# Float32 attention and gated feed-forward on one core: the even chunks of w_gate, their parts at two offsets in SBUF and their products in another order

## The chip, the cores and the metric

One core of a Trainium2 chip runs the whole program. The metric is the device time of one execution in microseconds; the median of three runs stands for the kernel. The profile comes from one further execution, whose own time is given beside its span.

## The reference

Attention with a mask by blocks of 64 positions (a query sees its own block and all earlier ones), then a feed-forward layer with a SiLU gate on its output, all compared in float32:

```python
# q, k, v: (8, 8, 576, 64); x: 4608 tokens of 512; w_gate, w_val: (512, 1536); w_out: (1536, 512)
scores = np.where(mask, scale * np.matmul(q, k.transpose(0, 1, 3, 2)), -1000000000.0)
attn = np.exp(scores - np.max(scores, axis=-1, keepdims=True))
attn = attn / (np.sum(attn, axis=-1, keepdims=True) + 1e-09)
x = np.matmul(attn, v)             # heads laid side by side: 4608 x 512
g = x @ w_gate
silu = g * (1.0 / (1.0 + np.exp(-g)))
out = (silu * (x @ w_val)) @ w_out
```

The weights arrive as float64.

## The kernel before

**Numbers in two parts.** TensorE multiplies here in the type fp32r, which keeps fewer bits than float32. So each factor is kept as a high part (the rounded value) and a low part (what rounding took off), and each product of the feed-forward layer is three matmuls into one PSUM sum: high weights by high x, high weights by low x, low weights by high x. In w_gate and w_val the weights are the stationary operand, loaded into the array before each matmul, and x is the moving one, streamed through it.

**Weights in SBUF (L200 to L212).** w_gate and w_val stay in SBUF for the whole run, cut into 12 chunks of 128 columns of d_ff. `g_odd` holds w_gate's odd chunks, `v_all` all of w_val, `g_even` w_gate's even chunks; each is a pair of tiles, number 0 for the high parts and number 1 for the low parts. A tile has 128 partitions, and along a partition 4 pieces d of the 512 input dimensions by its columns. `w_at(which, x, i)` gives part x of chunk i of w_gate (which = 0) or w_val (which = 1). Tiles take their places in the order of their calls. A tile of 64 bytes that nobody uses, `gap`, stands ahead of `g_even`. As it comes out, g_odd and v_all begin 64 bytes past a multiple of 128 (1984, 14272, 26560, 51136), both g_even tiles at a multiple of 128 (75776, 88064), and x's parts `xhl`, w_out's parts `wo` and the hidden layer's parts `hhl` too. Every step between the pieces that a matmul reads is a multiple of 128.

**The feed-forward loop.** Tokens are taken in 18 tiles of 256. For each tile, `feed_forward` walks over d_ff two chunks at a time, an even one and the odd one behind it. `up(i, 0, ...)` makes w_gate's products into one PSUM bank `gv`: 12 matmuls for the even chunk (y = 0; 4 pieces d, 3 matmuls each: L1105 high by high, L1106 high by low, L1107 low by high), then 12 for the odd one (y = 1). `up(i, 1, ...)` makes the same 24 for w_val into the other bank. ACT takes a tanh of the gate's sums (L1139), DVE makes the gated product (L1142 and the next) and ACT and DVE split it into `hhl` (L1152, L1155). The products with w_out (`down`, L1197 to L1199) are 12 matmuls of 512 columns into the sum `po`, with `hhl` stationary and `wo` moving. A turn of this loop is thus even 12, odd 12, value 24, w_out 12 (those of the turn before), with attention's matmuls (L569, L653, L782) between turns.

**The order of the work.** A planner in the kernel (`in_order`) gives every step an estimated cost and a rank and writes one fixed order for each engine. A step of `up` is one chunk's 12 matmuls from tile 4 on (`j >= FINE`); for tiles 0 to 3 it is the 3 matmuls of one d, so that other work can come between them, since weights and x are still being prepared. A step is placed only when its chunk's low part, the last thing made of a weight chunk (DVE, L986), and x's low part are done. Six pieces of w_out live for a time in w_gate's and w_val's tiles (`AWAY`) and are multiplied from there for tiles 0 and 1.

Of the kernel before, what the change touches and what calls it, by code (L numbers as in the profile page):

```python
# [7 lines left out]
F32 = mybir.dt.float32  # L8
F32R = mybir.dt.float32r
# [9 lines left out]
def kernel(  # L19
# [17 lines left out]
    nc = tc.nc  # L37
# [3 lines left out]
    P = 128  # L41
# [5 lines left out]
    NDC = DM // P  # L47
# [47 lines left out]
    const = ctx.enter_context(tc.tile_pool(name="const", bufs=1))  # L95
# [54 lines left out]
    def add(engine, cost, rank, fn, after=(), bufs=(), port=False, mode="", stage=""):  # L150


        t = Task(engine, cost, rank, fn, after, bufs, port, mode)
        for a in after:
            if a is not None:
                a.next.append(t)
                t.waits += 1
        for u in bufs:
            u.left += 1
        t.n, t.stage = len(tasks), stage  # L160
        tasks.append(t)
        return t
# [8 lines left out]
    def up_us(n):  # L171
        return n * 0.1134 + (0.012 if n < 3 * NDC else 0.0)
# [29 lines left out]
    half_w, whole_w = [P, NDC, DFF // 2], [P, NDC, DFF]  # L202
    g_odd = [const.tile(half_w, F32R, name=f"g_odd{x}") for x in range(2)]
    v_all = [const.tile(whole_w, F32R, name=f"v_all{x}") for x in range(2)]
    const.tile([P, 16], F32, name="gap")
    g_even = [const.tile(half_w, F32R, name=f"g_even{x}") for x in range(2)]

    def w_at(which, x, i):

        if which:  # L210
            return v_all[x][:, :, i * P : (i + 1) * P]
        return (g_odd if i % 2 else g_even)[x][:, :, i // 2 * P : (i // 2 + 1) * P]  # L212
# [101 lines left out]
    for i in range(7):  # L314
        n = 2**i
# [755 lines left out]
    def feed_forward(j, t0, w, xs):  # L1071
# [16 lines left out]
        def rank(i):  # L1088
            return (10.0 + (t0 + w * i / NFC) / S) if j > 1 else SIDE[j] + w * i / NFC / S

        def up(i, which, prev):

            ps = Buf("gv")
            ts = up_done[0]
            for y in range(2):

                for ds in [range(NDC)] if j >= FINE else [[d] for d in range(NDC)]:

                    def products(ds=ds, y=y):
                        hi, lo = (w_at(which, k, i + y) for k in range(2))  # L1100
                        o = ps[0][:, y * w : (y + 1) * w]
                        for d in ds:
                            xhi, xlo = (xs[d][1][k] for k in range(2))
                            first, last = d == 0, d == NDC - 1
                            nc.tensor.matmul(o, lhsT=hi[:, d], rhs=xhi[:, 0:w], start=first, stop=False)  # L1105
                            nc.tensor.matmul(o, lhsT=hi[:, d], rhs=xlo[:, 0:w], start=False, stop=False)  # L1106
                            nc.tensor.matmul(o, lhsT=lo[:, d], rhs=xhi[:, 0:w], start=False, stop=last)  # L1107

                    ts = add(
                        "PE",  # L1110
                        up_us(3 * len(ds)),
                        rank(i),
                        products,
                        [ts, *(xs[d][0] for d in ds), w_done[i + y, which]],
                        [ps, *(xs[d][1] for d in ds)],
                        stage="up",
                    )
                    ts.prev = prev
                    prev = ts if j >= FINE else None
            chain["up"] = up_done[0] = ts  # L1120
            return ps, ts

        for i in range(0, NFC, 2):
# [11 lines left out]
            n = 2 * w  # L1135
# [46 lines left out]
            every = [(y, m) for y in range(2) for m in range(nb)]  # L1182
# [273 lines left out]
```

## Time and profile before

| what | value |
|---|---|
| runs | 1172.72, 1174.53, 1175.42 us; median 1174.53 |
| profiled execution | 1178.6 us, span 1176.7 us, mean granted clock 0.991 |
| PE busy | 1149.6 us, 98% of the span, 8578 matmuls |
| weight loads (PEld) | 1029.6 us, 88%, 8578 |
| DVE, ACT, POOL busy | 746.6, 625.0, 322.1 us |
| DMA | 197.41 MB, mean 168 GB/s |

Rows of the profile name a line of the kernel, the engine, the operation and the tiles: `gv<-xhl,g_even` writes PSUM tile gv from x's parts and the weights g_even. Numbers of buffers are left out, so g_even stands for its high and its low tile. PE is the stream of matmuls, PEld the loads of their stationary operand, which run beside earlier matmuls. The length of a matmul's record includes its way through the array and overlaps that of the next, so PE's pace is read from one start to the next, not from lengths.

### The profile page before, as it was taken

Reading aid. Unit: us, or ns where it says so; the run is one execution under the profiler, and the core shown is the slowest. Engines: PE = TensorE matmul, PEld = TensorE weight load, DVE = VectorE, ACT = ScalarE, POOL = GpSimd, SP = SyncE. Lnnn points to the kernel's source line nnn. Section 1 sums busy time; section 2 is a strip of 40 time slices with the busy share of each in tenths; the row PEclk is TensorE's granted clock in tenths of the full one; section 3 lists DMA queues with packets and bytes.
Section 4 is the critical chain, followed back from the end, with each engine's and each line's share of the span. In section 5 each row is a group of like instructions: output and inputs, shape, how many; then the busy total and the mean of one; then the engine's idle time right before and its main releaser. Section 6 shows DMA issues by size and latency. Waiting matters only on the chain.

```text
span 1176.7 us, 21979 instructions
## 1 busy us (share of the span) xinstructions
PE 1149.6 (98%) x8578; PEld 1029.6 (88%) x8578; DVE 746.6 (63%) x1230; ACT 625.0 (53%) x1114; POOL 322.1 (27%) x139
## 2 busy tenths in 40 slices
PE   6889999999999999999999999999999999999998
PEld 5567878888899998989899998989989898999997
DVE  5798889677678574768567674856648565423222
ACT  5788877646383655637374564637355463212111
POOL 3212100144523333422414332342424233000000
PEclk8899999999999999999999999999999999999999
DMA  7666858756574646755376544745556434654442
GB/s 202 168 169 189 208 178 259 190 175 175 162 180 134 172 143 172 210 176 129 132 201 199 146 150 134 216 140 163 157 161 192 166 108 148 199 160 133 146 166 103
DMA packets 266984, 197.41 MB, mean 168 GB/s; under 512 B 195264, under 2 KB 231376, under 8 KB 266880
## 3 DMA queue, kind: packets, MB, share of 16 engines
q1 hardware_dynamic: 264304, 195.29, 56.8%
q8 instruction: 67, 1.10, 0.4%
q10 hardware_dynamic: 2576, 0.72, 0.3%
q14 instruction: 37, 0.30, 0.1%
HBM read 171.57 MB, written 24.38 MB: 167 GB/s over the span
## 4 chain that ended last, share of the span: by engine, by line
PE 90%; DVE 3%; ACT 3%; DMA 2%; issue 1%; SPq 0%; POOL 0%; ACTq 0%; POOLq 0%; DVEq 0%
PE gv L1105 17%; PE gv L1107 16%; PE gv L1106 16%; PE po L1197 8%; PE po L1198 7%; PE po L1199 7%; PE at L782 7%; PE at L569 5%; PE at L653 1%; PE at L1197 1%; PE at L442 1%; PE at L1198 1%; PE at L1199 1%; DVE mx L710 1%; DMA qk<-in_k_dram 1%
## 5 line engine op out<-in xcount | busy, mean ns | idle before, releaser
L714 POOL PARTITION_ALL_REDUCE mx<-mx x80 | 141.0, 1811 | 441.7 <-DVE mx L710 131.6
L833 POOL PARTITION_ALL_REDUCE mx<-mx x48 | 178.5, 3766 | 229.1 <-DVE mx L710 210.0
L1105 PE MATMUL gv<-xhl,v_all 128*128 128x256 f32 x864 | 241.0, 279 | 0.0
L1107 PE MATMUL gv<-xhl,v_all 128*128 128x256 f32 x864 | 239.2, 277 | 0.0
L1106 PE MATMUL gv<-xhl,v_all 128*128 128x256 f32 x864 | 239.0, 277 | 0.0
L1142 DVE SCALAR_TENSOR_TENSOR t<-t,gv 128x512 f32<-128x512 f32 x108 | 73.8, 684 | 146.6 <-ACT t L1139 146.0
L1105 PEld LDWEIGHTS gv<-xhl,v_all 128*128 128x128 f32 x864 | 162.1, 188 | 3.4 <-issue 2.1
L1106 PEld LDWEIGHTS gv<-xhl,v_all 128*128 128x128 f32 x864 | 162.3, 188 | 0.8
L1155 DVE TENSOR_TENSOR hhl<-t,hhl 128x512 fp32r<-128x512 f32 x108 | 91.4, 847 | 112.3 <-ACT hhl L1152 109.0
L1107 PEld LDWEIGHTS gv<-xhl,v_all 128*128 128x128 f32 x864 | 162.2, 188 | 0.1
L1152 ACT CAST hhl<-t 128x512 fp32r<-128x512 f32 x108 | 67.3, 623 | 156.2 <-PE po L1198 114.4
L1197 PE MATMUL po<-wo,hhl 128*128 128x512 f32 x372 | 148.3, 399 | 0.7 <-ACT ob L1224 0.7
L1198 PE MATMUL po<-wo,hhl 128*128 128x512 f32 x372 | 145.6, 391 | 0.0
L1199 PE MATMUL po<-wo,hhl 128*128 128x512 f32 x372 | 145.3, 390 | 0.0
L738 DVE TENSOR_TENSOR sc<-sc,mx 128x640 f32<-128x640 f32 (+6 forms) x168 | 123.4, 774 | 20.4 <-POOL mx L714 20.4
L1139 ACT ACTIVATE t<-gv 128x512 f32<-128x512 f32 x108 | 64.6, 598 | 119.6 <-PE gv L1107 116.9
L1105 PE MATMUL gv<-xhl,g_even 128*128 128x256 f32 x432 | 124.2, 288 | 0.2 <-DVE t L1142 0.2
L742 ACT ACTIVATE sc<-sc 128x1024 f32<-128x1024 f32 (+3 forms) x104 | 105.8, 1030 | 32.5 <-DVE sc L738 31.4
L1106 PE MATMUL gv<-xhl,g_even 128*128 128x256 f32 x432 | 122.5, 283 | 0.0
L1107 PE MATMUL gv<-xhl,g_even 128*128 128x256 f32 x432 | 122.3, 283 | 0.0
L1105 PE MATMUL gv<-xhl,g_odd 128*128 128x256 f32 x432 | 120.4, 279 | 0.0
L1107 PE MATMUL gv<-xhl,g_odd 128*128 128x256 f32 x432 | 119.5, 277 | 0.4 <-DVE g_odd L986 0.4
(175 smaller groups left out, 2398.8 us busy)
## 6 DMA issues: line engine op xcount, KB each, us to landing
wo<-wo_d SPq DMA_DIRECT2D x200, 512.0 KB
out_dram<-ob SPq DMA_DIRECT2D x35, 256.0 KB
v<-in_v_dram SPq DMA_DIRECT2D x64, 128.0 KB
xt<-x_d SPq DMA_DIRECT2D x64, 128.0 KB
rt<-r_d SPq DMA_DIRECT2D x128, 64.0 KB
qk<-in_q_dram SPq DMA_DIRECT2D x112, 72.0 KB
qk<-in_k_dram SPq DMA_DIRECT2D x104, 72.0 KB
x_d<-xu SPq DMA_DIRECT2D x24, 288.0 KB
```

Of the source, the lines that this page charges most:

```text
L714: nc.gpsimd.partition_all_reduce(m, m, channels=P, reduce_op=bass_isa.ReduceOp.max)
L738: nc.vector.tensor_tensor(piece(c), scores_of(c), m, ALU.subtract)
L742: nc.scalar.activation(x, x, AF.Exp)
L782: nc.tensor.matmul(ps[0][own(x), 1 - i if sums else i, q0 - s0 : s1 - s0], lhsT=ones if sums else vt[0][:, 2 * lane + c, own(x)], rhs=sc[0 ...
L833: nc.gpsimd.partition_all_reduce(m, m, channels=P, reduce_op=bass_isa.ReduceOp.add)
L1105: nc.tensor.matmul(o, lhsT=hi[:, d], rhs=xhi[:, 0:w], start=first, stop=False)
L1106: nc.tensor.matmul(o, lhsT=hi[:, d], rhs=xlo[:, 0:w], start=False, stop=False)
L1107: nc.tensor.matmul(o, lhsT=lo[:, d], rhs=xhi[:, 0:w], start=False, stop=last)
L1155: nc.vector.tensor_tensor(hh[1][:, 0:n], t[0][:, 0:n], hh[0][:, 0:n].bitcast(F32), ALU.subtract)
L1197: nc.tensor.matmul(po, lhsT=hi, rhs=whi, start=i + y == 0, stop=False)
L1198: nc.tensor.matmul(po, lhsT=hi, rhs=wlo, start=False, stop=False)
L1199: nc.tensor.matmul(po, lhsT=lo, rhs=whi, start=False, stop=i + y == NFC - 1)
```

## The change

The tiles of w_gate's even chunks change places, with two more 64-byte tiles between and behind them, and for the even chunks the third kind of matmul (low weights by high x) of all pieces d of a step goes ahead of the others:

```diff
     const.tile([P, 16], F32, name="gap")
-    g_even = [const.tile(half_w, F32R, name=f"g_even{x}") for x in range(2)]
+    low = const.tile(half_w, F32R, name="g_even1")
+    const.tile([P, 16], F32, name="gap1")
+    g_even = [const.tile(half_w, F32R, name="g_even0"), low]
+    const.tile([P, 16], F32, name="gap2")
...
-                        for d in ds:
-                            xhi, xlo = (xs[d][1][k] for k in range(2))
-                            first, last = d == 0, d == NDC - 1
-                            nc.tensor.matmul(o, lhsT=hi[:, d], rhs=xhi[:, 0:w], start=first, stop=False)
-                            nc.tensor.matmul(o, lhsT=hi[:, d], rhs=xlo[:, 0:w], start=False, stop=False)
-                            nc.tensor.matmul(o, lhsT=lo[:, d], rhs=xhi[:, 0:w], start=False, stop=last)
+                        low_first = which == 0 and y == 0
+                        every = [(d, x) for d in ds for x in range(3)]
+                        if low_first:
+                            every.sort(key=lambda p: p[1] < 2)
+                        for n, (d, x) in enumerate(every):
+                            first, last = ds[0] == 0 and not n, ds[-1] == NDC - 1 and n == len(every) - 1
+                            nc.tensor.matmul(
+                                o,
+                                lhsT=(lo if x == 2 else hi)[:, d],
+                                rhs=xs[d][1][int(x == 1)][:, 0:w],
+                                start=first,
+                                stop=last,
+                            )
```

The low tile now lies at 75776, a multiple of 128, the high tile at 88128, 64 bytes past one. g_odd and v_all stay where they were; everything behind g_even moves up by 128 bytes, so xhl, wo and hhl remain at multiples of 128. The costs and ranks that the planner works with are the same, and so is the order of all steps: on DVE, ACT, POOL and SP every instruction stands where it stood.

On PE the twelve matmuls of an even chunk change their order. This is the last even chunk of the last tile, before. Behind the arrow stand the moving tile (`xhl4_0` is the high part of x's first piece, `xhl4_1` its low part, and so on to xhl7) and the stationary one (g_even0 high, g_even1 low):

```order
L1105 MATMUL gv1_0_179<-xhl4_0_100,g_even0_76 128x256
L1106 MATMUL gv1_0_179<-xhl4_1_101,g_even0_76 128x256
L1107 MATMUL gv1_0_179<-xhl4_0_100,g_even1_77 128x256
L1105 MATMUL gv1_0_179<-xhl5_0_102,g_even0_76 128x256
L1106 MATMUL gv1_0_179<-xhl5_1_103,g_even0_76 128x256
L1107 MATMUL gv1_0_179<-xhl5_0_102,g_even1_77 128x256
L1105 MATMUL gv1_0_179<-xhl6_0_104,g_even0_76 128x256
L1106 MATMUL gv1_0_179<-xhl6_1_105,g_even0_76 128x256
L1107 MATMUL gv1_0_179<-xhl6_0_104,g_even1_77 128x256
L1105 MATMUL gv1_0_179<-xhl7_0_106,g_even0_76 128x256
L1106 MATMUL gv1_0_179<-xhl7_1_107,g_even0_76 128x256
L1107 MATMUL gv1_0_179<-xhl7_0_106,g_even1_77 128x256
```

And the same twelve places of the changed kernel, on PE too (all matmuls of `up` are now on L1111):

```order
L1111 MATMUL gv1_0_181<-xhl4_0_102,g_even1_76 128x256
L1111 MATMUL gv1_0_181<-xhl5_0_104,g_even1_76 128x256
L1111 MATMUL gv1_0_181<-xhl6_0_106,g_even1_76 128x256
L1111 MATMUL gv1_0_181<-xhl7_0_108,g_even1_76 128x256
L1111 MATMUL gv1_0_181<-xhl4_0_102,g_even0_78 128x256
L1111 MATMUL gv1_0_181<-xhl4_1_103,g_even0_78 128x256
L1111 MATMUL gv1_0_181<-xhl5_0_104,g_even0_78 128x256
L1111 MATMUL gv1_0_181<-xhl5_1_105,g_even0_78 128x256
L1111 MATMUL gv1_0_181<-xhl6_0_106,g_even0_78 128x256
L1111 MATMUL gv1_0_181<-xhl6_1_107,g_even0_78 128x256
L1111 MATMUL gv1_0_181<-xhl7_0_108,g_even0_78 128x256
L1111 MATMUL gv1_0_181<-xhl7_1_109,g_even0_78 128x256
```

The four low weights have moved to the front, one after the other; the eight with high weights follow in their old order.

In tiles 0 to 3, where a step has one d, the move stays within three matmuls. Two such steps that follow each other on PE, of tile 0 (pieces d = 1 and 2), before:

```order
L1105 MATMUL gv0_0_157<-xhl1_0_94,g_even0_76 128x256
L1106 MATMUL gv0_0_157<-xhl1_1_95,g_even0_76 128x256
L1107 MATMUL gv0_0_157<-xhl1_0_94,g_even1_77 128x256
L1105 MATMUL gv0_0_157<-xhl2_0_96,g_even0_76 128x256
L1106 MATMUL gv0_0_157<-xhl2_1_97,g_even0_76 128x256
L1107 MATMUL gv0_0_157<-xhl2_0_96,g_even1_77 128x256
```

The same two steps on PE in the changed kernel:

```order
L1111 MATMUL gv0_0_159<-xhl1_0_96,g_even1_76 128x256
L1111 MATMUL gv0_0_159<-xhl1_0_96,g_even0_78 128x256
L1111 MATMUL gv0_0_159<-xhl1_1_97,g_even0_78 128x256
L1111 MATMUL gv0_0_159<-xhl2_0_98,g_even1_76 128x256
L1111 MATMUL gv0_0_159<-xhl2_0_98,g_even0_78 128x256
L1111 MATMUL gv0_0_159<-xhl2_1_99,g_even0_78 128x256
```

Here the low weights come as every third, one ahead of two with high weights.

## The prediction

> **What bounds the kernel now.** I start with the busy time by stretch, then the chain of work that ended last.
>
> ```profile
> 0.00:350.00 350.00, 326.56 (x2475) 271.16 (x2476) 272.69 (x488) 247.25 (x443) 93.33 (x62) 0.97 0.68 187
> 350.00:1000.00 650.00, 650.00 (x4872) 596.99 (x4871) 422.05 (x655) 344.35 (x611) 228.80 (x78) 1.00 0.55 162
> 1000.00:1177.00 177.00, 173.01 (x1235) 161.49 (x1233) 51.91 (x89) 33.42 (x61) 0.00 (x0) 1.00 0.46 151
> ```
>
> Behind each stretch's length stand PE, PEld, DVE, ACT and POOL with their instructions, then the granted clock and the DMA share. PE lacks 23.4 us of the first 350, nothing of the next 650, and at the end only the tail. DVE (422 of 650) and ACT (344) have room.
>
> ```profile
> PE 90%; DVE 3%; ACT 3%; DMA 2%; issue 1%; SPq 0%; POOL 0%; ACTq 0%; POOLq 0%; DVEq 0%
> ```
>
> So from 350 us on, a nanosecond off a product's pace comes off the end. A busy sum says nothing of that pace, since products overlap; what counts is the distance from start to start. One turn of the loop over w_gate and w_val late in the kernel (start, length, in us):
>
> ```profile
> 1068.29 0.28 PE L1105 MATMUL gv<-xhl,g_even 128*128 128x256 f32 x1
> 1068.40 0.28 PE L1106 MATMUL gv<-xhl,g_even 128*128 128x256 f32 x1
> 1068.52 0.28 PE L1107 MATMUL gv<-xhl,g_even 128*128 128x256 f32 x1
> 1068.64 0.28 PE L1105 MATMUL gv<-xhl,g_even 128*128 128x256 f32 x1
> 1068.76 0.28 PE L1106 MATMUL gv<-xhl,g_even 128*128 128x256 f32 x1
> ...
> 1069.60 0.28 PE L1107 MATMUL gv<-xhl,g_even 128*128 128x256 f32 x1
> 1069.72 0.28 PE L1105 MATMUL gv<-xhl,g_odd 128*128 128x256 f32 x1
> ...
> 1071.08 0.28 PE L1105 MATMUL gv<-xhl,v_all 128*128 128x256 f32 x1
> ...
> 1073.80 0.40 PE L1197 MATMUL po<-wo,hhl 128*128 128x512 f32 x1
> ```
>
> The twelve products of the even chunk take 1069.72 - 1068.29 = 1.43 us, the twelve of the odd one 1.36, the 24 of w_val 2.72. In steady state that is (1069.60 - 1068.52) / 9 = **0.120 us** a product with even weights and 2.72 / 24 = **0.1133** with the others. Shapes, moving tiles and instruction counts are the same; what differs is where the weights lie: g_even at a multiple of 128 bytes, as the moving xhl do, g_odd and v_all 64 past one. It holds throughout (count | busy us, mean ns; from 350 us on):
>
> ```profile
> L1107 PE MATMUL gv<-xhl,v_all 128*128 128x256 f32 x681 | 188.2, 276 | 0.0
> L1107 PE MATMUL gv<-xhl,g_even 128*128 128x256 f32 x340 | 96.2, 283 | 0.0
> L1107 PE MATMUL gv<-xhl,g_odd 128*128 128x256 f32 x340 | 93.8, 276 | 0.0
> ```
>
> 340 of each of three products are 85 groups of twelve.
>
> **The pace has a memory.** If it were the address alone, all even weights would simply be moved by 64 bytes. But here a value group follows w_out's products with no even chunk between:
>
> ```profile
> 836.33 0.39 PE L1199 MATMUL po<-wo,hhl 128*128 128x512 f32 x1
> 836.55 0.28 PE L1105 MATMUL gv<-xhl,v_all 128*128 128x256 f32 x1
> ...
> 839.38 0.28 PE L1105 MATMUL gv<-xhl,g_even 128*128 128x256 f32 x1
> ...
> 839.85 0.28 PE L1106 MATMUL gv<-xhl,g_even 128*128 128x256 f32 x1
> ...
> 840.80 0.28 PE L1105 MATMUL gv<-xhl,g_odd 128*128 128x256 f32 x1
> L1106 PE MATMUL gv<-xhl,v_all 128*128 128x256 f32 x8 | 2.2, 279 | 0.0
> L1106 PE MATMUL gv<-xhl,v_all 128*128 128x256 f32 x8 | 2.2, 276 | 0.0
> ```
>
> It takes 839.38 - 836.55 = 2.83 us, 0.1179 a product, to its end: the weights 64 past the multiple have a **slow pace** too, and nothing inside the group ends it. (The last two rows are that group, mean 279 ns, and the one at 1071 us, 276.) The even chunk, slow as it is, puts the array into the state in which the 36 products behind it run at 0.1133. That is worth 36 x 0.0046 = 0.166 us a turn, more than the chunk itself can give. How many aligned products this takes decides the case. In the weight loads of the group at 1068.3 us (mean ns), the first three rows are its loads 2 to 4, the fourth three of its later ones:
>
> ```profile
> L1106 PEld LDWEIGHTS gv<-xhl,g_even 128*128 128x128 f32 x1 | 0.2, 188 | 0.0
> L1107 PEld LDWEIGHTS gv<-xhl,g_even 128*128 128x128 f32 x1 | 0.2, 188 | 0.0
> L1105 PEld LDWEIGHTS gv<-xhl,g_even 128*128 128x128 f32 x1 | 0.2, 192 | 0.0
> ...
> L1106 PEld LDWEIGHTS gv<-xhl,g_even 128*128 128x128 f32 x3 | 0.6, 192 | 0.0
> ```
>
> The steady mark of the aligned state, a load of 192 ns and a step of 0.12, is there with the fourth load. Behind attention's products it comes one later; the last two rows here are that group's fourth and fifth load:
>
> ```profile
> 452.24 0.28 PE L569 MATMUL at<-parts,parts 128*128 128x192 f32 x1
> 452.36 0.30 PE L1105 MATMUL gv<-xhl,g_even 128*128 128x256 f32 x1
> ...
> 452.85 0.28 PE L1106 MATMUL gv<-xhl,g_even 128*128 128x256 f32 x1
> ...
> 453.81 0.28 PE L1105 MATMUL gv<-xhl,g_odd 128*128 128x256 f32 x1
> ...
> L1105 PEld LDWEIGHTS gv<-xhl,g_even 128*128 128x128 f32 x1 | 0.2, 188 | 0.0
> L1106 PEld LDWEIGHTS gv<-xhl,g_even 128*128 128x128 f32 x1 | 0.2, 192 | 0.0
> ```
>
> Behind a slow group three are not enough:
>
> ```profile
> 137.01 0.28 PE L1105 MATMUL gv<-xhl,g_even 128*128 128x256 f32 x1
> ...
> 137.37 0.28 PE L1105 MATMUL gv<-xhl,v_all 128*128 128x256 f32 x1
> ...
> 138.07 0.28 PE L1105 MATMUL gv<-xhl,v_all 128*128 128x256 f32 x1
> ```
>
> Six value products take 0.70 us there, 0.117 each: still slow.
>
> **The change part by part.** No instruction is added or removed, and the order on DVE, ACT, POOL and SP stays. The four low products of an even chunk go first and stay aligned; the eight high ones follow with weights 64 past the multiple.
>
> Whole groups behind w_out's or attention's products: by the starts in the timeline 82 of the 85 stand so or behind a group of quick pace. Today the fifth product starts 1068.76 - 1068.29 = 0.47 us into the group. If four aligned ones set the state, the other eight run at 0.1133, 0.907 in all: 1.377 in place of 1.43, **0.053 saved**. Behind attention the same sum is 0.49 + 0.907 against 453.81 - 452.36 = 1.45, again 0.053. 82 x 0.053 = 4.35 us. PE waits for nothing here, so all of it should reach the end; the wait next in line is that for DVE's and ACT's part of each turn, which follows PE's pace with a third of its time free.
>
> Three of the 85 follow a slow value group (one is the row at 839.38). Its even group is not steady by the fifth product, so I let the pace stay slow: the eight cost 0.943 instead of 840.80 - 839.85 = 0.95, and the 36 behind them 0.166 more. 3 x 0.16 = 0.48 us lost.
>
> Tiles 0 to 3, before 350 us, issue their products by d, in threes: now low, high, high, never four aligned in a row.
>
> ```profile
> L1106 PE MATMUL gv<-xhl,v_all 128*128 128x256 f32 x184 | 51.3, 279 | 0.0
> L1106 PE MATMUL gv<-xhl,g_even 128*128 128x256 f32 x92 | 26.3, 286 | 0.0
> L1106 PE MATMUL gv<-xhl,g_odd 128*128 128x256 f32 x92 | 25.5, 278 | 0.0
> ```
>
> 92 groups of three, so 184 products get the new place. No row shows such a mixture. Best, all run quick: 184 x 0.0067 = 1.2 us saved. Worst, none of them sets the state: 184 x 0.0021 = 0.4 saved, and the products that are quick today turn slow; the means (278 and 279, where quick is 276 and slow 279) leave at most a third of the 276 odd and 552 value products quick, some 276 x 0.0046 = 1.3 lost: 0.9 on balance. The nearest row is the short group at 137 us, which set nothing, so I take a loss of 0.4.
>
> First uses of a chunk: the first product now waits for the low part, which DVE makes last. The scheduler already issues a group only behind that part, so I cost it at nothing; at the most a few tenths for six chunks, in the stretch that has 23.4 us of idle time. The 128 bytes by which everything behind the gaps moves leave every remainder by 128 as it was: nothing, if 128 is the period; that rests on no row, and I hold it as a rival.
>
> Sum: -4.35 + 0.48 + 0.4 = **-3.5 us**. The profiled execution took 1178.6 us (span 1176.7) and would take 1175.1; the median shown is 1174.53, which gives **1171.0**.
>
> A rule against all this: the Trainium skill (SBUF — State Buffer, Who interferes with whom) gives PE two independent read ports, one for the moving operand and one for weights, and says that PE waits for nobody. By it the place of the weights could not matter and the time would stay at 1174.5. This trace disagrees: 283 against 276 ns for the same product, by the tile that holds its weights.
>
> **Rivals.** (1) *Four aligned products do not set the state*, as three did not at 137 us. Then the eight run at 0.1179 (0.943, the group 1.413, 0.017 saved) and the 36 behind lose 0.166: 0.149 a turn, 82 x 0.149 = 12.2, with 0.48 and 0.9 some 13.6 us: **1188**, slower. It decides if more than four are needed; for it speaks the group at 839.38, against it the mark of 192 ns at the fourth load. Chance 0.14. (2) *They set it behind w_out, not behind attention*, where the mark comes one load later: 15 groups by the timeline. 67 x 0.053 - 15 x 0.149 = 1.3 saved, less 0.9 and 0.5: **1174.5**, no change. 0.09. (3) *The place has no such effect*: the period is longer than 128, or the difference belongs to something else about the chunk; the high products stay at 0.120 or trade it for another cost. **1174.5**. 0.08. For it: no row has weights at other distances from xhl. (4) *The quick pace spreads*: with less time spent in the aligned state the early groups and the three behind slow ones run quick as well, 4.35 + 1.2 = 5.6 saved, and of the slow early products a share (each third of 828 x 0.0046 is 1.3 us): **1168 to 1169**. No early row speaks for it. 0.08.
>
> **How the numbers follow.** The forecast has 0.61; between the bounds of the early groups it alone spans 4.35 - 0.48 + 1.2 = 5.1 saved, 1169.4, and 4.35 - 0.48 - 0.9 = 3.0 saved, 1171.6. What can be told from no change is 0.2%, 2.35 us: faster below 1172.2, slower above 1176.9. Nearly all of the forecast and (4) are faster: 0.66; (2), (3) and the forecast's rim are the same: 0.20; (1) is slower: 0.14. The range from 1168.0 to 1175.5 leaves out (1) and little else.
>
> **What would show it.** Right: in the late timeline an even group of 1.38 us with steps of 0.12 over its low products only, the odd one behind it still 1.36 and value groups 2.72, mean ns of g_even's rows some 278. Wrong by (1): value groups of 2.83 and means of 279 everywhere. By (2): 2.83 only behind attention. By (3): the even group still 1.43 with 283. PE's busy time should stay the whole of the stretch; an idle time there would mean that another engine came due.

## The result, and the profile after

| kernel | median us (runs) | ratio to before, 95% interval |
|---|---|---|
| before | 1175.51 (14) | |
| changed | 1177.74 (14) | 1.0018, 1.001 to 1.0025 |

The change costs 2.2 us, between 1.2 and 2.9 by the interval. (The 1174.53 us from which the forecast counts was the median of three of these runs of before.) The forecast was a gain of 3.5, and the time lies above the range.

The two profiled executions don't show it by their spans: 1176.6 us after, 1176.7 before. The busy times by stretch show why (columns as before: stretch, its length, busy time and instructions of PE, PEld, DVE, ACT and POOL, granted clock, DMA share and GB/s):

```profile
0.00:350.00 350.00, 326.88 (x2496) 272.27 (x2497) 273.09 (x489) 247.50 (x444) 95.59 (x63) 0.98 0.69 189
350.00:1000.00 650.00, 650.00 (x4851) 596.77 (x4851) 420.80 (x653) 342.99 (x609) 226.50 (x77) 1.00 0.56 161
1000.00:1177.00 177.00, 172.89 (x1234) 161.27 (x1232) 52.08 (x89) 33.47 (x61) 0.00 (x0) 1.00 0.46 151
```

PE is still busy for all of the middle stretch. But it had issued 2496 products at 350 us, 21 more than before, and yet ended level: this execution was ahead by some 2.4 us in its loading phase and gave them back. Over the 14 profiled executions of this study the time to the same product in that phase varies by 7 us (344.05 to 351.23). So from here on kernels are compared by their **late part**: from the end of the product that runs at 350 us in the trace of before (the same product, by its number in PE's order, in every kernel) to the end of the last one. It takes 822.96 us before and 825.23 after, 2.27 more, which is about the difference of the medians, 2.23.

Where they are spent stands in the rows by line of the late part of the changed kernel (count | busy us, mean ns):

```profile
L1111 PE MATMUL gv<-xhl,v_all 128*128 128x256 f32 x2040 | 247.6, 277 | 0.0
L1111 PE MATMUL gv<-xhl,g_even 128*128 128x256 f32 x1008 | 133.5, 281 | 0.0
L1111 PE MATMUL gv<-xhl,g_odd 128*128 128x256 f32 x1012 | 129.6, 277 | 0.0
```

g_even's mean should have come to 278 and is 281; the two others have gone from 276 to 277. As in the prediction, the pace itself is read from starts. A turn behind w_out, in the timeline (start, length):

```profile
1059.68 0.40 PE L1209 MATMUL po<-wo,hhl 128*128 128x512 f32 x1
1059.91 1.59 PE L1111 MATMUL gv<-xhl,g_even 128*128 128x256 f32 x12
1061.34 1.52 PE L1111 MATMUL gv<-xhl,g_odd 128*128 128x256 f32 x12
1062.70 2.88 PE L1111 MATMUL gv<-xhl,v_all 128*128 128x256 f32 x24
1065.42 0.40 PE L1207 MATMUL po<-wo,hhl 128*128 128x512 f32 x1
```

The even group takes 1061.34 - 1059.91 = 1.43 us as it did before, the odd one 1.36, the value group 2.72. And one behind attention:

```profile
933.06 0.28 PE L572 MATMUL at<-parts,parts 128*128 128x192 f32 x1
933.18 1.60 PE L1111 MATMUL gv<-xhl,g_even 128*128 128x256 f32 x12
934.61 1.58 PE L1111 MATMUL gv<-xhl,g_odd 128*128 128x256 f32 x12
936.02 2.99 PE L1111 MATMUL gv<-xhl,v_all 128*128 128x256 f32 x24
938.85 0.30 PE L572 MATMUL at<-qk,parts 128*128 128x288 f32 x1
```

There the odd group takes 1.41 and the value group 2.83: slow. The steps from product to product inside the even groups say more. The steps, and the mean lengths and sums by group further on, are worked out from the records' ends, from the end of one product to the end of the next; the start steps tell the same within 4 ns. In ns, for a late turn behind w_out (after: the one at 1059.91; the last two columns are the groups behind it):

```
                 even group, 12 steps                                odd    value
before           115 118 120 120 120 120 120 120 120 120 120 120    1361   2722
after            123 122 121 118 118 118 119 116 118 119 117 117    1361   2721
```

Before, all steps settle at 120. After, neither part of the group does what the forecast wanted: the four low products run at 118 to 123 and never come to the steady 120, and the eight high ones behind them run at the slow pace of 118, not at 113.3. As I read it, the low products no longer put the array into the state; the odd and the value group behind them run quick in this turn all the same.

### The profile page after: what moved, and what is told of

Its sections match the earlier page's. It is cut to its first block, busy times and chain, and to the rows that moved or that the text cites. A ratio compares the mean times of both kernels' runs of the same rounds, so it can differ in the third digit from the quotient of the medians.

```text
span 1176.6 us, 21979 instructions
## 1 busy us (share of the span) xinstructions
PE 1149.8 (98%) x8578; PEld 1030.3 (88%) x8578; DVE 746.0 (63%) x1230; ACT 624.0 (53%) x1114; POOL 322.1 (27%) x139
## 4 chain that ended last, share of the span: by engine, by line
PE 88%; ACT 4%; DVE 3%; DMA 2%; issue 1%; SPq 1%; POOL 0%; POOLq 0%; DVEq 0%; ACTq 0%
PE gv L1111 48%; PE po L1207 8%; PE po L1209 7%; PE po L1208 7%; PE at L785 7%; PE at L572 6%; DMA wo<-in_moe_w_out_dram 2%; PE at L656 1%; DVE mx L713 1%; PE at L1207 1%; ACT sc L463 1%; ACT ob L967 1%; PE at L1209 1%; PE at L1208 1%; PE at L445 1%
## 5 line engine op out<-in xcount | busy, mean ns | idle before, releaser
L1111 PE MATMUL gv<-xhl,v_all 128*128 128x256 f32 x2592 | 322.7, 278 | 0.0
L1111 PEld LDWEIGHTS gv<-xhl,v_all 128*128 128x128 f32 x2592 | 308.8, 188 | 4.3 <-issue 2.1
L1111 PE MATMUL gv<-xhl,g_even 128*128 128x256 f32 x1296 | 176.7, 283 | 0.2 <-DVE t L1152 0.2
L1111 PEld LDWEIGHTS gv<-xhl,g_even 128*128 128x128 f32 x1296 | 167.8, 189 | 8.6 <-issue 1.6
L1111 PE MATMUL gv<-xhl,g_odd 128*128 128x256 f32 x1296 | 169.5, 278 | 0.4 <-DVE g_odd L989 0.4
L1152 DVE SCALAR_TENSOR_TENSOR t<-t,gv 128x512 f32<-128x512 f32 x108 | 73.7, 682 | 147.1 <-ACT t L1149 146.6
L1111 PEld LDWEIGHTS gv<-xhl,g_odd 128*128 128x128 f32 x1296 | 158.3, 188 | 3.2 <-issue 1.7
L1157 DVE SCALAR_TENSOR_TENSOR t<-t,gv 128x512 f32<-128x512 f32 x108 | 73.7, 683 | 62.0 <-PE gv L1111 60.9
L713 DVE TENSOR_TENSOR mx<-mx,sc 128x128 f32<-128x128 f32 (+2 forms) x180 | 100.4, 564 | 2.1 <-ACT sc L477 0.3
L785 PE MATMUL at<-sc,v 128*64 128x320 f32 (+4 forms) x868 | 92.2, 367 | 0.1
L582 ACT ACTIVATE sc<-at 128x576 f32<-128x576 f32 x80 | 66.9, 838 | 44.8 <-PE at L572 42.0
```

The costliest lines, as they stand in the source:

```text
L713: nc.vector.tensor_tensor(into, prev, of(c), op)
L785: nc.tensor.matmul(ps[0][own(x), 1 - i if sums else i, q0 - s0 : s1 - s0], lhsT=ones if sums else vt[0][:, 2 * lane + c, own(x)], rhs=sc[0 ...
L1111: nc.tensor.matmul(o, lhsT=(lo if x == 2 else hi)[:, d], rhs=xs[d][1][int(x == 1)][:, 0:w], start=first, stop=last,)
L1152: nc.vector.scalar_tensor_tensor(t[0][:, 0:n], t[0][:, 0:n], 1.0, pg[0][:, 0:n], ALU.add, ALU.mult)
```

## The experiments

**What they were to tell apart.** One number of the layout had been left out of the prediction. Everything behind g_even moved by 128 bytes, xhl too, while g_odd, v_all and the place where g_even begins stayed. Let the *distance* be the address of the weights less that of xhl, modulo 256. Before, it is 0 for both even tiles and 192 for g_odd and v_all. After, it is 128 for the low tile, 192 for the high one and 64 for g_odd and v_all. If the period is 256 bytes and not 128, the low weights have lost their alignment (B in the expectations). Against this stood two other readings: that the four products do not suffice wherever they lie, and that the new order of the products costs something by itself (C).

The table has the changed kernel and the twelve of the experiments. "Late" is the difference of the late part to before's. "Before" is the kernel before, run beside them on the same chip. In all of them xhl moves together with wo and attention's tiles (with hhl too, but for E7 and E8). That the distance which counts is the one to xhl, the moving operand of the same product, is thus argued from its part in the product; no run moves xhl alone.

| kernel | distance low / high / odd and value | low products | us (runs) | before | ratio, 95% interval | late, us |
|---|---|---|---|---|---|---|
| changed | 128 / 192 / 64 | first | 1177.74 (14) | 1175.51 | 1.0018, 1.001 to 1.0025 | +2.27 |
| E1 | 0 / 192 / 192 | first | 1172.02 (9) | 1175.67 | 0.9967, 0.9957 to 0.9978 | -3.46 |
| E2 | 0 / 0 / 192 | first | 1175.49 (10) | 1175.67 | 0.9997, 0.9988 to 1.0006 | 0.00 |
| E3 | 128 / 128 / 64 | every third | 1177.49 (10) | 1175.67 | 1.0019, 1.0009 to 1.0029 | +1.89 |
| E4 | 192 / 192 / 192 | every third | 1185.47 (4) | 1175.67 | 1.0088, 1.0073 to 1.0103 | +9.66 |
| E5 | 0 / 0 / 192 | every third | 1175.25 (10) | 1175.70 | 0.9999, 0.999 to 1.0009 | 0.00 |
| E6 | 128 / 192 / 192 | first | 1188.87 (4) | 1175.70 | 1.0115, 1.01 to 1.013 | +13.87 |
| E7 | 0 / 192 / 192, hhl 64 past | first | 1189.86 (4) | 1175.70 | 1.0118, 1.0103 to 1.0133 | +12.19 |
| E8 | 192 / 192 / 192, hhl 64 past | every third | 1190.27 (4) | 1175.70 | 1.0126, 1.0109 to 1.0143 | +13.38 |
| E9 | 0 / 192 / 64 | first | 1171.38 (7) | 1175.82 | 0.9963, 0.9952 to 0.9975 | -4.13 |
| E10 | 0 / 192 / 224 and 160 | first | 1189.60 (4) | 1175.82 | 1.011, 1.0086 to 1.0135 | +12.34 |
| E11 | 0 / 192 / 32 and 96 | first | 1189.31 (4) | 1175.82 | 1.011, 1.0091 to 1.013 | +12.90 |
| E12 | 0 / 192 / 64 | last | 1188.68 (4) | 1176.21 | 1.0101, 1.0084 to 1.0118 | +10.73 |

**E1: the change without the move of the tail.** The high tile takes the place ahead of the old gap, the low one the place behind it; xhl and all else stay where they were. Order as in the change.

```diff
+    high = const.tile(half_w, F32R, name="g_even0")
     const.tile([P, 16], F32, name="gap")
-    g_even = [const.tile(half_w, F32R, name=f"g_even{x}") for x in range(2)]
+    g_even = [high, const.tile(half_w, F32R, name="g_even1")]
```

> The changed order, but the high tile of the even chunks goes ahead of the old 64-byte gap and the low tile behind it, so that everything behind them stays at its address of before: high weights 64 past a multiple of 128, low weights at one, and no tile elsewhere moves. Theory A (the pace depends on the remainder by 128 alone, and four aligned low products are too few to set the quick state): the same picture as in the changed kernel, even group behind w_out 1.426 us, turns behind attention slow (value groups 2.83 us), time about 2 us above before. Theory B (the remainder by 256 or more counts, and the 128-byte move of everything behind the gaps spoiled the state): the forecast comes true here, even groups 1.38 us, odd 1.36, value 2.72 behind w_out and behind attention, some 3.5 to 4.5 us below before.

Measured: 3.65 us faster. The timeline of E1, a late turn behind w_out:

```profile
1148.44 1.54 PE L1109 MATMUL gv<-xhl,g_even 128*128 128x256 f32 x12
1149.82 1.52 PE L1109 MATMUL gv<-xhl,g_odd 128*128 128x256 f32 x12
1151.18 2.88 PE L1109 MATMUL gv<-xhl,v_all 128*128 128x256 f32 x24
1153.90 0.40 PE L1205 MATMUL at<-wo,hhl 128*128 128x512 f32 x1
```

Even 1.38, odd 1.36, value 2.72: the turn that was forecast for the change. Its steps are 116 118 119 120 and then 113 to 114 eight times. So four aligned products set the state, and places alone make the difference between a gain of 3.65 us and a loss of 2.23. The two kernels differ in the 128 bytes of the tail and in which of the two even tiles comes first; E6 and E9 keep E1's order of the tiles and change the distances alone.

**E2: the order alone**, in the layout of before. **E3: the move alone**, in the order of before:

```diff
     g_even = [const.tile(half_w, F32R, name=f"g_even{x}") for x in range(2)]
+    const.tile([P, 32], F32, name="gap2")
```

> The changed order on the layout of before: low products first, all even weights at a multiple of 128, nothing moved. Theory A and theory B: the order alone does nothing, even group 1.43 us, odd 1.36, value 2.72, time within 0.1% of before. A third theory C (it is the order that spoils the state, since four low products by four high parts of x follow each other): the first step of the even group is 124 ns and not 115, and turns behind attention are slow, 2 us above before.

> The order and the places of before, but 128 unused bytes behind the even chunks' tiles, so that everything behind them (xhl, wo, hhl and the rest) moves by 128 bytes: the remainders by 128 stay, those by 256 change. Theory A: nothing changes, 1.43, 1.36 and 2.72 us, time within 0.1% of before. Theory B: the even chunk no longer sets the quick state everywhere, and turns behind attention run slow (odd 1.413, value 2.83 us), 15 x 0.16 = 2.4 us or more above before.

E2 measured no change, and its late part is equal to before's to 0.01 us: the order is free as long as all twelve are aligned. E3, 128 bytes that nobody uses, costs 1.82 us. Its even groups take 1.448 us behind w_out in the mean, against 1.433 before, and settle nowhere (124 121 121 118 121 121 118 ...). The way in which it was to lose missed: I had looked for slow odd and value groups behind attention, 2.4 us or more, and in all turns there but one the odd group took 1.37 and the value group 2.72.

**E4: no aligned weights at all.** The gap goes behind both even tiles; order of before.

```diff
-    const.tile([P, 16], F32, name="gap")
     g_even = [const.tile(half_w, F32R, name=f"g_even{x}") for x in range(2)]
+    const.tile([P, 16], F32, name="gap")
```

> The order of before, and both even tiles ahead of the 64-byte gap: all of w_gate and w_val 64 past a multiple of 128, nothing behind them moved. Both theories, by the memory that the prediction read off the slow value group: no aligned products are left to set the quick state, so every turn is slow, even 1.415, odd 1.415, value 2.83 us, 0.15 us a turn over 85 turns, some 12 us above before. If the pace had no memory: every group quick, 1.36 for the even ones, 85 x 0.07 = 6 us below before.

The timeline of E4, a late turn behind w_out (the first product of each group):

```profile
1157.03 0.28 PE L1105 MATMUL gv<-xhl,g_even 128*128 128x256 f32 x1
...
1158.44 0.28 PE L1105 MATMUL gv<-xhl,g_odd 128*128 128x256 f32 x1
...
1159.86 0.28 PE L1105 MATMUL gv<-xhl,v_all 128*128 128x256 f32 x1
...
1162.68 0.40 PE L1197 MATMUL at<-wo,hhl 128*128 128x512 f32 x1
```

1.41, 1.42 and 2.82 us: every product at 118 ns. Whoever moves all the weights off the alignment to be rid of the 120 loses the 113 too, in nearly all turns, and pays 9.8 us, of some 12 expected. The memory of the pace is shown.

**E5: 256 bytes instead of E3's 128.**

```diff
+    const.tile([P, 64], F32, name="gap2")
```

> Order and places of before, with 256 unused bytes behind the even chunks' tiles where the shift by 128 had 128. Theory B1 (the period of the effect is 256 bytes): every group as in before, even 1.433 us behind w_out, odd 1.361, value 2.721, w_out 2.775, time within 0.1% of before. Theory B2 (the period is 512 or more): groups other than before's, as the shift by 128 gave (even 1.447, odd 1.365), or worse.

No change, and the sum of every kind of product in the late part is what it was before, to 0.01 us. One row of E3 and the same of E5, by line in the late part:

```profile
L1108 PE MATMUL gv<-xhl,g_even 128*128 128x256 f32 x339 | 96.4, 285 | 0.0
```

```profile
L1108 PE MATMUL gv<-xhl,g_even 128*128 128x256 f32 x337 | 95.3, 283 | 0.0
```

283 is what before has. A move by 128 counts, one by 256 doesn't: **the period is 256 bytes.**

**E6: E1 with the low tile at distance 128**, xhl at its old remainder by 256.

```diff
-    const.tile([P, 16], F32, name="gap")
-    g_even = [const.tile(half_w, F32R, name=f"g_even{x}") for x in range(2)]
+    high = const.tile(half_w, F32R, name="g_even0")
+    const.tile([P, 48], F32, name="gap")
+    g_even = [high, const.tile(half_w, F32R, name="g_even1")]
+    const.tile([P, 32], F32, name="gap2")
```

> The faster kernel of the first four (low first, everything behind at its place), but the low tile 128 bytes further and everything behind it 256 further: low weights at a distance of 128 from xhl by the remainder by 256, high, odd and value weights at 192 as in before. It takes one of the changed kernel's two differences alone. If the low parts' distance of 128 is what keeps the quick state from being set: even group 1.426 us behind w_out with a first step of 124 ns and the high products at 117.7 ns, as in the changed kernel, and perhaps slow turns behind attention. If it is the distance of 64 of the odd and value weights: even group 1.38 us, odd 1.36, value 2.72 in all turns, 3 to 4 us below before. (Both hold only if the period is 256.)

The timeline of E6, a late turn behind w_out:

```profile
1162.70 1.59 PE L1110 MATMUL gv<-xhl,g_even 128*128 128x256 f32 x12
1164.13 1.57 PE L1110 MATMUL gv<-xhl,g_odd 128*128 128x256 f32 x12
1165.54 2.99 PE L1110 MATMUL gv<-xhl,v_all 128*128 128x256 f32 x24
1168.37 0.40 PE L1206 MATMUL at<-wo,hhl 128*128 128x512 f32 x1
```

1.43, 1.41 and 2.83. The steps of the even group, 125 120 121 118 118 118 119 117 ..., are those of the changed kernel. So low weights at distance 128 do not set the state. But E6 loses 13.2 us and the changed kernel 2.2: there, g_odd and v_all lie at 64, and behind w_out they run quick all the same.

**E7 and E8: the hidden layer.** E7 is E1, E8 is E4, each with hhl, the stationary operand of w_out's products, 64 bytes further (distance 64 to wo instead of 0).

```diff
     for tag, variant in first_of:
+        if tag == "hhl":
+            const.tile([P, 16], F32, name="gap3")
...
+    const.tile([P, 48], F32, name="gap4")
```

> The faster kernel of the first four, with the hidden layer's parts hhl 64 past a multiple of 128, so that w_out's products get weights 64 past their moving operand too; tiles behind hhl move by 256. Those twelve take 2.775 us now, 231 ns each, where the quickest single ones take 226.7. If the distance acts on them as on the others: up to 12 x 4.5 = 54 ns a group, over 86 groups 4.6 us below that kernel. If 512 columns hide it, or w_out's products have a slow state of their own: w_out's group unchanged or longer, and as the state that they leave is another, the four low products may no longer set the quick one, in which case turns are slow, 8 to 12 us more.

> The kernel with all of w_gate and w_val 64 past a multiple of 128 and no low-first order, with hhl moved likewise. It asks whether the slow state comes from w_out's aligned products. If it does (w_out leaves the array in a state from which weights at 64 run slow): every group quick, even 1.36, odd 1.36, value 2.72 us, 6 us below before for the even chunks and up to 4.6 for w_out, some 10 us. If weights at 64 past start slow behind anything: as without hhl's move, some 10 us above before.

Both lose. The timeline of E7, a late turn (the first of w_out's twelve products, the three groups behind them, the next of w_out's):

```profile
1162.82 0.39 PE L1208 MATMUL at<-wo,hhl 128*128 128x512 f32 x1
...
1165.62 1.57 PE L1112 MATMUL gv<-xhl,g_even 128*128 128x256 f32 x12
1167.02 1.57 PE L1112 MATMUL gv<-xhl,g_odd 128*128 128x256 f32 x12
1168.43 2.99 PE L1112 MATMUL gv<-xhl,v_all 128*128 128x256 f32 x24
1171.26 0.39 PE L1208 MATMUL at<-wo,hhl 128*128 128x512 f32 x1
```

Odd 1.41 and value 2.83: slow. In the mean over the late part w_out's twelve products take 2.82 us instead of 2.77, which is 4.3 of E7's 12.2 us. The rest is the turns behind them: in E7, with E1's weights in E1's order, the low products there run at 115 113 117 120 and the groups behind at 118. Behind attention the same groups run quick in E7 (odd 1.364, value 2.730 in the mean) and even in E8 (1.364 and 2.729), where nothing is aligned. One such turn of E8 (the first product of each group, and attention's next):

```profile
960.23 0.30 PE L1108 MATMUL gv<-xhl,g_even 128*128 128x256 f32 x1
...
961.61 0.28 PE L1108 MATMUL gv<-xhl,g_odd 128*128 128x256 f32 x1
...
962.97 0.28 PE L1108 MATMUL gv<-xhl,v_all 128*128 128x256 f32 x1
...
965.69 0.30 PE L572 MATMUL at<-qk,parts 128*128 128x288 f32 x1
```

So the state that the work ahead leaves counts as well as the first products of a group.

**E9: the low tile moved with xhl.** E1 with 128 unused bytes ahead of the high tile, so that the distances are 0, 192 and 64. With E1, E6 and the changed kernel it makes a square of two by two.

```diff
+    const.tile([P, 32], F32, name="gap1")
+    high = const.tile(half_w, F32R, name="g_even0")
     const.tile([P, 16], F32, name="gap")
-    g_even = [const.tile(half_w, F32R, name=f"g_even{x}") for x in range(2)]
+    g_even = [high, const.tile(half_w, F32R, name="g_even1")]
```

> The changed kernel's other difference alone: low parts at distance 0 and high parts at 192 as in the faster kernel, but 128 more bytes ahead of both, so that the odd and value weights stand at 64 from xhl. With low at 128 they are the two differences of the changed kernel; the four combinations are then complete. If the low parts at 0 set the quick state whatever the others' distance: even 1.38 us, odd and value quick in all turns, 3 to 4 us below before. If the step from 192 to 64 between the even and the odd chunk disturbs the state: odd and value groups slow behind w_out or behind attention, and the time at or above before.

| late part against before, us | odd and value at 192 | at 64 |
|---|---|---|
| low at 0 | -3.46 (E1) | -4.13 (E9) |
| low at 128 | +13.87 (E6) | +2.27 (changed) |

With the low tile at 128 the late part is longer in both columns, by 17.33 us at 192 and by 6.40 at 64. E9 is the fastest version found, 4.4 us below before. All four are the same instructions in the same order; E6 and E9 differ by 17.5 us through places alone. E9 also mends the turns behind a slow value group. First E9, then E1 at the same place of the program:

```profile
830.99 2.99 PE L1110 MATMUL gv<-xhl,v_all 128*128 128x256 f32 x24
833.82 1.55 PE L1110 MATMUL gv<-xhl,g_even 128*128 128x256 f32 x12
835.21 1.52 PE L1110 MATMUL gv<-xhl,g_odd 128*128 128x256 f32 x12
836.57 2.88 PE L1110 MATMUL gv<-xhl,v_all 128*128 128x256 f32 x24
839.29 0.40 PE L1206 MATMUL po<-wo,hhl 128*128 128x512 f32 x1
```

```profile
832.98 2.99 PE L1109 MATMUL gv<-xhl,v_all 128*128 128x256 f32 x24
835.80 1.57 PE L1109 MATMUL gv<-xhl,g_even 128*128 128x256 f32 x12
837.21 1.57 PE L1109 MATMUL gv<-xhl,g_odd 128*128 128x256 f32 x12
838.62 2.99 PE L1109 MATMUL gv<-xhl,v_all 128*128 128x256 f32 x24
841.45 0.40 PE L1205 MATMUL po<-wo,hhl 128*128 128x512 f32 x1
```

Behind the slow value group (2.83 and 2.82 us) E9's turn is 1.39, 1.36 and 2.72, E1's 1.41, 1.41 and 2.83.

**E10 and E11: other distances for g_odd and v_all**, in E1's layout otherwise, in search of one that is quick behind anything. E10 (E11's sizes are 24, 16 and 24):

```diff
+    const.tile([P, 8], F32, name="gap1")
     g_odd = [const.tile(half_w, F32R, name=f"g_odd{x}") for x in range(2)]
+    const.tile([P, 48], F32, name="gap2")
     v_all = [const.tile(whole_w, F32R, name=f"v_all{x}") for x in range(2)]
+    const.tile([P, 8], F32, name="gap3")
+    high = const.tile(half_w, F32R, name="g_even0")
```

> The faster kernel with the odd chunks' weights at a distance of 224 from xhl (by the remainder by 256) and w_val's at 160, even chunks as they were, everything behind moved by one whole period of 256. It asks for the pace at distances that are no multiple of 64. If only whole 64-byte lines count, 224 acts as 192 and 160 as 128: odd 1.361 us, value products 120 ns each (2.88 us), some 13 us above before. If the pace falls off evenly with the distance, odd and value lie between 1.36 and 1.43, 2.72 and 2.86. If one of the two is quick behind anything, its group is quick also where value groups were slow, behind w_out without an even chunk.

> The same with the odd weights at 32 and w_val's at 96. If only whole 64-byte lines count, 32 acts as 0 (odd 1.43 us, 120 ns a product) and 96 as 64 (value 2.72 us): some 6 us above the faster kernel, 2 to 3 above before. If a distance between is quick behind anything, its group stays at 113.3 ns a product in the three turns in which value groups were slow, too.

None is. Behind an even group of 1.385 us a product takes, in ns: 117.1 at distance 224, 119.7 at 160 (E10), 118.7 at 32, 118.8 at 96 (E11). Only 64 and 192 reach 113.3. I had hoped for a rule from these four, and there is none simple: 224 is neither like its neighbour 192 nor like 0.

**E12: E9 with the four low products last.** One word of E9's order is another:

```diff
-                            every.sort(key=lambda p: p[1] < 2)
+                            every.sort(key=lambda p: p[1] == 2)
```

> The fastest kernel so far (low at 0, high at 192, odd and value at 64), with the four low products of the even chunk last instead of first. Theory (weights at 64 and 192 run at the pace of the state that they meet, and about four products with weights at 0 set the quick one): behind w_out the eight high products run slow, 117.8 ns each, the four low ones some 119, so the even group takes 1.42 us and saves almost nothing, while the odd and value groups behind them stay quick, 1.36 and 2.72 us: about 1 us below before, 3 us above the low-first order. If the order were of no account for the high products: 1.38 us, 4 us below before. If the low ones must stand behind w_out to set the state: odd and value groups slow, 10 us or more above before.

The timeline of E12, a late turn behind w_out:

```profile
1165.24 1.58 PE L1110 MATMUL gv<-xhl,g_even 128*128 128x256 f32 x12
1166.65 1.58 PE L1110 MATMUL gv<-xhl,g_odd 128*128 128x256 f32 x12
1168.07 2.99 PE L1110 MATMUL gv<-xhl,v_all 128*128 128x256 f32 x24
1170.89 0.39 PE L1206 MATMUL at<-wo,hhl 128*128 128x512 f32 x1
```

1.41, 1.42 and 2.82 us. The last four steps of the even group are 121 118 119 118 or 121 118 120 117, not 120: four aligned products behind eight at 118 ns set nothing, though the layout is that of the best kernel. The theory of the expectation, that about four set the state wherever they stand, is refuted. Nor is it the slow pace ahead alone: E9's four set the state behind a slow value group, whose weights are at 64, and E1's don't behind one at 192, where E12's eight are too. The order, free in E2, is worth 17 us here.

## Why the prediction was wrong

**The step that failed** is this one: "The 128 bytes by which everything behind the gaps moves leave every remainder by 128 as it was: nothing, if 128 is the period; that rests on no row, and I hold it as a rival". It was costed at nothing in the sum. By E5 and E3 the period is 256, and by E1 against the changed kernel this step is worth 1177.74 - 1172.02 = 5.7 us, or 2.23 + 3.65 = 5.9 with each beside its own runs of before. The square says which of the two distances that it moved did the harm, if the distances are all that counts (the changed kernel's own three with the high tile first were not run): the low tile's. E9 has odd and value at 64 as the changed kernel has and gains 4.13 in the late part; with the low tile at 128 that is a loss of 2.27, so 6.40 us, where the late part misses the forecast by 2.27 + 3.87 = 6.14. It was also priced wrongly as a rival: I put "longer than 128" together with "no effect" at 1174.5. What a period of 256 does could have been worked out from the addresses that were at hand: the low tile at 128, thus not aligned, and g_odd and v_all at 64, which no row showed. A term resting on no row needed a bound on both sides; E6 and E9 show how far apart they are, 1171 to 1189.

**By the terms of the late part:**

| term | forecast, us | E1 (tail kept) | changed |
|---|---|---|---|
| even groups | -4.35 | -4.30 | -0.88 |
| odd and value groups | +0.48 | +0.74 | +2.66 |
| w_out's products | 0 | +0.10 | +0.46 |
| sum of the late part | -3.87 | -3.46 | +2.27 |

The 0.03 us that the last column's sum has beyond its terms are attention's products.

- *PE sets the end from 350 us on*: right. It is busy in all of the middle stretch in every kernel of the table, and late differences of -4 to +14 us come out at the end.
- *The pace has a memory, so that the even weights can't all be moved by 64 bytes*: right (E4, +9.8 us).
- *Four aligned products set the state, seen by the mark of 192 ns*: right behind w_out and behind attention, if they are aligned by 256 (E1: 1.381 and 1.403 us). The mark is there too: in E1's late turns behind w_out the loads 4 and 5 take 192 ns, in its slow turn at 835.80 none takes more than 189. Rival 1, that four do not suffice, holds where something stands ahead that the prediction had not priced: behind slow products at distance 192 (E12, E1 at 835.80) and behind w_out's with hhl moved (E7).
- *Three groups behind slow value groups lose*: two of them do in E1 (at 659.31 and 835.80), and two turns that were not counted, one behind attention (470.55) and one behind six of w_out's products (739.30); together +0.74 for the 0.48 forecast. In the changed kernel other groups lose more.
- *The order itself, and first uses*: right, nothing (E2).
- *Tiles 0 to 3 lose 0.4*: not settled. The loading phase varies by more from one execution to the next. The medians less the late parts leave -0.04 us for the changed kernel and -0.19 for E1, with intervals of about 1 us.
- *Rival 2*: its picture, slow turns behind attention alone, is what the trace shows for odd and value groups. But its cause was another (a mark one load later), and E1, where the groups behind attention are quick in all turns but the one at 470.55, refutes that. Its even groups behind w_out were to be 1.38 and are 1.43.

The rule that was weighed there, two independent read ports of PE and no waiting, from the Trainium skill (SBUF — State Buffer, Who interferes with whom), read as leaving the place of the weights no effect, does not hold for this pace. By that reading E6 and E9 would take the same time. They take 1188.87 and 1171.38 us, 13.2 above and 4.4 below before.

**What stays open.** What the "state" is in the hardware was not found. Nor is it known why behind w_out, in the changed kernel, g_odd and v_all at 64 come out of a slow even group at the quick pace, while behind attention they don't, nor why w_out's own products, with hhl and wo at their old distance, gain and lose up to 1.8 us in the late part (-0.70 in E4, +0.46 in the changed kernel, +1.75 in E6). Whether distances to xhl alone count, and not those to other tiles that moved with it, no run shows. The runs give a table of places and not its reason.

## What to carry to other kernels

Where back-to-back products differ in pace by the place of a tile alone, write down the distance of each stationary operand from its moving one, before and after, by the largest period that the rows do not exclude, and remember that a tile inserted anywhere moves all behind it. Test a period by unused bytes: one run with half of it and one with all of it (E3, E5) would have shown that the open term was not nothing. And compare a turn's groups behind each kind of work that can stand ahead of it, since a pace can be inherited.

## What the runs showed of the hardware

- The pace of 256-column fp32r products from the same instructions depends on the places of the tiles, as far as the runs go on the distance between weights and moving tile, modulo 256 bytes: 120 ns at 0, 118 to 125 at 128 behind w_out, 113.3 or 118 at 64 and 192 by the state they meet, 117 to 120 at 32, 96, 160 and 224. 128 unused bytes cost 1.89 us in the late part (E3), 256 nothing (E5).
- The state lasts over at least the 36 products behind. Four products at distance 0 set it behind w_out or attention (E1, E9), but not behind w_out with hhl moved (E7), nor behind products of 118 ns at 192 (E12; E1 at 835.80), while behind such products at 64 they do (E9 at 833.82). At distance 128 they don't when the others are at 192 (E6); with odd and value weights at 64 these run quick behind w_out even so (the changed kernel, 1.36 and 2.72 us).
- w_out's products of 512 columns have such a pace too: moving hhl 64 bytes off its distance of 0 to wo made twelve of them 2.82 us instead of 2.77, and left a state in which the next turn is slow (E7, E8).
